# Requesting nine of fourteen weight pieces behind the gather of expert 0, and another order of the first low halves

## The chip, the cores and the metric
The kernel runs on one core of a Trainium2 chip. The metric is the device time of one execution in microseconds (us). The core has five engines that run their own instruction streams side by side: TensorE (PE, with its weight loads shown as PEld), VectorE (DVE), ScalarE (ACT), GpSimd (POOL) and SyncE (SP). SP issues most of the DMAs here; all its loads go into one hardware queue in the order in which it issues them.

## The reference
Three stages in a row, all in float32:

```
# gated linear attention, B=2, H=8, S=768, D=48
state = alpha[t] * state + outer(k[t], v[t]);  y[t] = q[t] @ state
x = y as [1536 tokens, 384]

# mixture of experts, top 1 of 8, capacity 384
logits = x @ w_gate;  e = argmax(logits)
gate = exp(logits - max) / (sum + 1e-9)      # of the chosen expert
h = relu(rows_of_expert @ w1[e])             # 384 -> 1024
out[token] = gate * (h @ w2[e])              # 1024 -> 384

# feed-forward
h = out @ w_in                               # 384 -> 2048
g = h * tanh(softplus(h))
result = g @ w_out                           # 2048 -> 384
```

## The kernel before
**Attention** runs in 12 tiles of 128 tokens. As tiles end, POOL scatters their token rows (1,536 B each) into a table `tab` in DRAM, sorted by expert (line 108). `gather(e)` (lines 120 to 128) then asks SP for the first 240 rows of expert e's part of the table, in two transfers of 128 and 112 rows (line 124); it waits for the scatters. For expert 0 the gather is issued before the last two tiles are scattered; their rows are put in by TensorE (`slot_mm`, `slot_rest`).

**The expert loop** has 64 steps, 8 experts with 8 blocks of 128 hidden units each. Step s does `g1` of block s (9 matmuls, line 1063: high half of the weights by high half of the rows, low by high, high by low), ScalarE and VectorE split the result into `hh` and `hl` (lines 1067, 1068), and `g2` of the block three steps back follows (9 matmuls, line 1080). At block 5 of each expert `xpose` turns the next expert's rows (TensorE, line 1035, straight behind that step's `g2`), and the gather of the expert after that is asked for.

**The weights** come in pieces of 384 KB, numbered in the order of use: an even piece is `w1` for two blocks, an odd piece `w2` for the same two. Blocks 0 and 1 use pieces 0 and 1, blocks 4 and 5 pieces 4 and 5. Each goes through three steps: `load_to` asks SP for it (line 331) into one of 14 buffers, `conv_high` makes its high half `whi` on ScalarE (line 343), `conv_low` its low half `wlo` on VectorE (line 349: piece minus high half). The weights of the feed-forward come as 64-bit words; `cvt_load` asks for them in 512 KB loads (line 225), the first three of them between the end of attention and the expert loop, and ScalarE and VectorE turn them in spare moments of the loop.

**What sets the order** around the change. The program order is the order of each engine's queue. The table `PRE` says how many pieces are asked for by the end of each attention tile; at tile 11 the lines `load_to(PRE[i])`, `conv_high(1)`, `gather(0)`, `load_to(14)` follow each other. `conv_high(n)` itself asks for pieces up to `ahead[0]` beyond the one it converts. Behind attention come the three `cvt_load`s, the rows of expert 0, the scatter of the last tile and `gather(1)`; requests that `conv_high` makes there stand between them. In the loop, each step calls `conv_high` and `conv_low`; `low` is the list of pieces whose high half is done and low half is not. `places()` computes on VectorE where each expert's tokens begin and `sort_places()` each token's place; POOL scatters the token numbers (`toks`) to these places later.

Of the kernel before, what the change touches and what calls it, by code (L numbers as in the profile page):

```python
# [23 lines left out]
def kernel(  # L24
# [22 lines left out]
    E = w1.shape[0]  # L47
# [18 lines left out]
    ATT = 4  # L66
# [4 lines left out]
    LEAD = 6  # L71
    WST = 6
# [11 lines left out]
    def w_new(i):  # L84
        p = wr_p[2 if i >= 76 else (i + 8) % 12 < 8]
        whi[i], wlo[i] = (p.tile([128, PW], F32R, tag=t, name=f"{t}{i}") for t in ("whi", "wlo"))
# [99 lines left out]
    NP1 = 2 * FF // 256  # L186
# [35 lines left out]
    def cvt_load(n):  # L222
        if n < len(cvt_jobs):
            t = words(fpool[0].tile([128, 2 * CN], F32, tag="big", name="w64", bufs=3)[:, 0:2 * cvt_jobs[n][1].shape[1]])
            nc.sync.dma_start(out=t, in_=words(cvt_jobs[n][0]))
            cvt_t[n] = [t]
# [39 lines left out]
    def late_load(n):  # L266
        if not 0 <= n < NLATE:
            return
        st = late_pool(n).tile([128, PW], F32, tag="st", name=f"sd{n}")
        fs = slice(FH + n // 2 * 128, FH + (n // 2 + 1) * 128)  # L270
        if n % 2:
            nc.sync.dma_start(out=words(st), in_=words(w_out[fs, :]))
        else:
            nc.sync.dma_start(
                out=st.bitcast(U32).rearrange("p (k f) -> p k f", k=KD),
                in_=w_in.bitcast(U32)[:, 2 * fs.start:2 * fs.stop].rearrange("(k p) f -> p k f", p=128),
            )
        late_t[n] = st
# [39 lines left out]
            hi, lo, w = late_t.pop(n)[3:]  # L318
            nc.vector.tensor_tensor(out=lo, in0=w, in1=hi.bitcast(F32), op=ALU.subtract)

    ahead = [WST + 4]
    conv_n, load_n, cvt_n = [0], [0], [0]

    def written(i):
# [2 lines left out]
    def load_to(n):  # L327
        while load_n[0] < min(n, len(pieces)) and cvt_n[0] >= written(load_n[0]):
            i = load_n[0]
            st = raw_p[i % 14 >= 8].tile([128, PW], F32, tag="st", name=f"st{i}")  # L330
            nc.sync.dma_start(out=st.rearrange("p (a b) -> p a b", b=pieces[i].shape[2]), in_=pieces[i])
            wst_t[i] = st
            load_n[0] += 1

    low = []

    def conv_high(n):
        while conv_n[0] < min(n, len(pieces)):
            i = conv_n[0]
            load_to(i + 1 + ahead[0])  # L340
            w = wst_t.pop(i)
            w_new(i)
            nc.scalar.activation(out=whi[i], in_=w, func=AF.Copy)  # L343
            low.append((i, w))
            conv_n[0] += 1

    def conv_low(n=None):
        for i, w in low[:n]:
            nc.vector.tensor_tensor(out=wlo[i], in0=w, in1=whi[i].bitcast(F32), op=ALU.subtract)  # L349
        del low[:n]  # L350

    def conv_to(n):
        conv_high(n)
        conv_low()
# [10 lines left out]
    with ExitStack() as actx:  # L365
# [135 lines left out]
        def decay_check(i):  # L501
            j1 = sp.tile([128, HP, C], F32, tag="junk", name="junk", bufs=1)
            nc.scalar.activation(
                out=j1[0:R2], in_=er_t.pop(i)[0:R2], func=AF.Square, bias=neg1[0:R2], accum_out=chk[0:R2, i:i + 1]
            )
# [254 lines left out]
        def route_c(i):  # L760
            xg = xg_t.pop(i)
            scatter(tab, si_all[:, i:i + 1], xg.rearrange("p j d -> p (j d)"), E * NT, "tab")
# [58 lines left out]
        def slot_mm(i, ks=range(KD)):  # L821
            x = xg_l[i - SLOT1].rearrange("p j d -> p (j d)")
            for kk in ks:
                t = feat(0, WIN)[kk]
                nc.tensor.matmul(  # L825
                    out=t, lhsT=x[:, kk * 128:(kk + 1) * 128], rhs=hot_t[i], start=(i == SLOT1 and kk % 2 == 0),
                    stop=(i == NTILE - 1), skip_group_check=True,
                )
# [63 lines left out]
            for f in (route_lg, route_max, route_exp, route_idx, route_hot):  # L892
                f(i)

        PRE = {5: 1, 6: 3, 7: 5, 8: 8, 9: 11, 10: 12, 11: 12}
        EXP = {4: groups[0], 7: groups[1], 9: groups[2]}
        HOT = {5: groups[0], 7: groups[1], 9: groups[2]}
        RANK = {6: groups[0], 8: groups[1], 10: groups[2]}
        for i in range(1, NTILE - 1):
# [63 lines left out]
            if not far:  # L963
                route_x(i - 1)
                route_c(i - 1)
            load_to(PRE.get(i, 0))
        i = NTILE - 1
# [21 lines left out]
        decay_check(i)  # L989
        load_to(PRE[i])  # L990
        conv_high(1)
        gather(0)
        load_to(14)
        i = NTILE - 1
# [15 lines left out]
        count(i + 1)  # L1010
        route_c(SLOT1)
        conv_high(ATT - 1)
        conv_low(1)
        low.reverse()
        slot_mm(NTILE - 1)
        del xs_t[0]
        tot = rk[:, E:2 * E]
# [38 lines left out]
    def g1(e, m):  # L1056
        xh, xl = xt_e[e]
        wh, wl = w_first(e, m)
        hps = bk[2 + m % 2][:, m // 2 % 2 * WB:m // 2 % 2 * WB + WIN]
        n = 0  # L1060
        for a, b_ in ((wh, xh), (wl, xh), (wh, xl)):
            for kk in range(KD):
                nc.tensor.matmul(out=hps, lhsT=a[:, kk], rhs=b_[:, kk, :], start=(n == 0), stop=(n == 3 * KD - 1))  # L1063
                n += 1
        hh = fp.tile([128, WIN], F32R, tag="hh", name="hh", bufs=LAG + 1)
        hl = fp.tile([128, WIN], F32R, tag="hl", name="hl", bufs=LAG + 1)
        nc.scalar.activation(out=hh, in_=hps, func=AF.Relu)  # L1067
        nc.vector.scalar_tensor_tensor(  # L1068
            out=hl, in0=hps, scalar=0.0, in1=hh.bitcast(F32), op0=ALU.max, op1=ALU.subtract
        )  # L1070
        h_t[e, m] = (hh, hl)

    def g2(e, m):
        y = feat(4 + e % 2 * 2, WIN)
        hh, hl = h_t.pop((e, m))
        wh, wl = w_second(e, m)
        for n in range(KD):
            ns = slice(n * 128, (n + 1) * 128)
            for t, (a, b_) in enumerate(((wh, hh), (wl, hh), (wh, hl))):
                nc.tensor.matmul(  # L1080
                    out=y[n], lhsT=a[:, ns], rhs=b_, start=(m == 0 and t == 0 and n % 2 == 0),
                    stop=(m == MF - 1 and t == 2), skip_group_check=True,
                )
# [15 lines left out]
    def y_out(e):  # L1099
        y_put(4 + e % 2 * 2, off_v.pop(e), free=e == E - 1)  # L1100

    def tok_scatter(i):
        scatter(toks, pos_i[:, i:i + 1], tokid[:, i:i + 1], NT)

    def place(col, engines=DYN):
        return nc.values_load(meta_i[0:1, col:col + 1], engines=engines, min_val=0, max_val=NT)
# [8 lines left out]
    def slow_at():  # L1115
        nc.vector.scalar_tensor_tensor(
            out=slow_f, in0=mxc[0:1], scalar=float(WIN), in1=bad, op0=ALU.is_gt, op1=ALU.max
        )
# [113 lines left out]
    def at(n):  # L1232
        return steps[n] if 0 <= n < NS else None


    def f_mish(n, between=None):
# [22 lines left out]
        if n % 2:  # L1259
            late_low(late - 2)  # L1260
            late_join(late - 1)
            late_load(late + LATE_AHEAD - 1)
        conv_to(E * MF - EARLY + n + LEAD)

# [35 lines left out]
        part(last, cs[3], True)  # L1300

    EARLY = LAG2
    for n in range(3):
        cvt_load(n)
    CVT_END = 45
    LATE_AHEAD = 3
    xpose(0, False)
    nc.vector.tensor_reduce(out=mxc, in_=tot, axis=AX.X, op=ALU.max)
    conv_low(1)
    conv_high(ATT)  # L1310
    scatter(tab, si_last, xg_last, E * NT, "tab")
    gather(1)
# [6 lines left out]
    for e in range(E):  # L1319
        for m in range(MF):  # L1320
            step = e * MF + m
            if m == 6:
                off_v[e] = place(e)
            g1(e, m)
            pend.append((e, m))
            if len(pend) > LAG:
                pe, pm = pend.pop(0)
                g2(pe, pm)
                if pm == MF - 1:
                    y_out(pe)  # L1330
            if e == E - 1 and m >= MF - EARLY:
                n = m - MF + EARLY
                (f_head if m < MF - 1 else f1_at)(n)
            conv_high(min(step + 1 + LEAD, ATT + step * 9 // 8, E * NP1 + 3))
            conv_low(None if step > 2 else min(step, 1))
            for f, n in job_at.get(step, ()):
                f(n)
                if f is cvt_b:
                    cvt_load(n + 3)
            if step == 3:  # L1340
                check_all(cm)
                slow_at()
            if step == 1:
                places()
            if step == 2:
                sort_places()
            if step % 4 == 3 and 0 < step // 4 <= NTILE:
                tok_scatter(step // 4 - 1)
            if e == E - 1 and m == 0:
                nc.sync.dma_start(  # L1350
                    out=srt, in_=toks.rearrange("(c p) o -> p (c o)", p=128), allow_slow_non_contiguous=True
                )
            if E * MF - EARLY - 1 - LATE_AHEAD <= step < E * MF - EARLY - 1:
                late_load(step - (E * MF - EARLY - 1 - LATE_AHEAD))
            if step == E * MF - 4:
                cvt_marks()
            if step == E * MF - 2:
                cvt_flag()
            if m == 5 and e + 1 < E:
                xpose(e + 1)  # L1360
                if e + 2 < E:
                    gather(e + 2)
    for pe, pm in pend:
        g2(pe, pm)
    apart.append(at(EARLY))
    f1(at(EARLY))
# [239 lines left out]
```

## Time and profile before

| | |
|---|---|
| median of 3 runs | 425.91 us (425.75 to 427.06) |
| the profiled execution | 426.99 us, its span 424.8 us |
| TensorE busy | 409.5 us, 96% of the span |
| VectorE busy | 324.7 us, 76% |
| ScalarE busy | 324.5 us, 76% |
| DMA, mean over the span | 158 GB/s |

The profile is of one execution; the span is from the first to the last instruction, and 2.2 us of the execution lie around it. Attention ends and the expert loop begins at about 80 us. A window row gives for a stretch the busy time of each engine, the clock that TensorE was granted (1.00 is 2.4 GHz, 0.50 is 1.2 GHz), the mean busy share of the 16 DMA engines (it can come out a little over 1) and the rate. In a timeline, a row with xN groups N instructions in a row, and brackets give the idle time of the engine before it and what ended it.

### The profile page before, as it was taken

What the parts mean: (1) busy time and instruction counts of PE and PEld (TensorE: products, weight loads), DVE (VectorE), ACT (ScalarE), POOL (GpSimd) and SP (SyncE); (2) the same over time, 40 slices, a digit from 0 to 9 for tenths busy, and PEclk for the clock granted to TensorE, in tenths of its full rate; (3) what the DMA queues carried; (4) which work ended last, traced back from release to release, by engine and by line L of the source; (5) the groups of instructions that cost most, each with busy time, mean ns of one, the idle gap of its engine ahead of it and who ended that gap; (6) DMA issues with size and microseconds to landing.
All of it is one profiled execution on the core that took longest, in us unless ns stands there. A gap on an engine that the chain in (4) does not pass through costs nothing.

```text
span 424.8 us, 8347 instructions
## 1 busy us (share of the span) xinstructions
PE 409.5 (96%) x3110; PEld 377.2 (89%) x3112; DVE 324.7 (76%) x643; ACT 324.5 (76%) x571; POOL 59.8 (14%) x76
## 2 busy tenths in 40 slices
PE   7899998989999999999999999999999999999993
PEld 3798977889999999999988989898989998889893
DVE  7999985699898988988749877966796675565451
ACT  5889977667778776877679988788878878797640
POOL 5222564221120111100000000000000000002033
PEclk9999997899999999999999999999999999999998
DMA  8999995799999999971552300112110000001022
GB/s 237 350 291 329 363 378 186 248 294 299 320 315 275 295 280 322 279 238 27 179 181 71 115 1 0 39 41 72 37 39 3 0 2 0 0 2 75 2 76 79
DMA packets 50541, 67.31 MB, mean 158 GB/s; under 512 B 5372, under 2 KB 41212, under 8 KB 50492
## 3 DMA queue, kind: packets, MB, share of 16 engines
q1 hardware_dynamic: 48572, 61.97, 48.1%
q0 software_dynamic: 1920, 4.73, 3.0%
q8 instruction: 26, 0.43, 0.4%
q14 instruction: 23, 0.19, 0.1%
HBM read 55.86 MB, written 10.83 MB: 157 GB/s over the span
## 4 chain that ended last, share of the span: by engine, by line
PE 91%; DVE 3%; issue 1%; ACT 1%; POOL 1%; DMA 1%; SPq 0%; POOLq 0%; DVEq 0%; ACTq 0%
PE bk L1144 24%; PE bk L1187 23%; PE bk L1080 15%; PE bk L1063 15%; PE bk L526 3%; PE bk L572 3%; PE bk L588 3%; PE bk L561 2%; PE bk L540 1%; PE bk L1035 1%; PE bk L596 1%; DMA kn<-in_k_t_dram 1%; DVE wlo L349 1%; PE bk L825 1%; POOL st__990 L531 0%
## 5 line engine op out<-in xcount | busy, mean ns | idle before, releaser
L349 DVE TENSOR_TENSOR wlo<-st,whi 128x768 fp32r<-128x768 f32 x72 | 68.3, 954 | 13.1 <-ACT whi L343 10.8
L1187 PE MATMUL bk<-whi,big 128*128 128x384 f32 x240 | 66.4, 337 | 0.0
L1172 DVE TENSOR_TENSOR p<-p,bk 128x512 f32<-128x512 f32 x48 | 32.8, 683 | 43.2 <-ACT p L1162 43.2
L343 ACT ACTIVATE whi<-st 128x768 fp32r<-128x768 f32 x72 | 60.1, 840 | 0.0
L1156 ACT ACTIVATE p<-bk 128x512 f32<-128x512 f32 x48 | 28.8, 599 | 31.9 <-PE bk L1144 28.6
L1080 PE MATMUL bk<-hl,whi 128*128 128x240 f32 x192 | 52.9, 276 | 0.0
L1080 PE MATMUL bk<-hh,wlo 128*128 128x240 f32 x192 | 52.7, 275 | 0.0
L1080 PE MATMUL bk<-hh,whi 128*128 128x240 f32 x192 | 52.7, 274 | 0.0
L1187 PEld LDWEIGHTS bk<-whi,big 128*128 128x128 f32 x240 | 44.1, 188 | 1.5
L108 POOL DMA_INDIRECT out_dram<-acc,srt x12 | 12.2, 1017 | 235.0 <-DVE acc L1211 230.6
L1067 ACT ACTIVATE hh<-bk 128x240 fp32r<-128x240 f32 x64 | 23.5, 368 | 28.3 <-PE bk L1063 28.3
L1144 PE MATMUL bk<-x2l,whi 128*128 128x512 f32 x144 | 41.6, 397 | 0.0
L1144 PE MATMUL bk<-x2h,wlo 128*128 128x512 f32 x144 | 41.2, 394 | 0.0
L1144 PE MATMUL bk<-x2h,whi 128*128 128x512 f32 x144 | 41.1, 394 | 0.0
L1187 PE MATMUL bk<-wlo,big 128*128 128x384 f32 x120 | 40.6, 338 | 0.0
L1080 PEld LDWEIGHTS bk<-hl,whi 128*128 128x128 f32 x192 | 36.4, 189 | 0.2 <-DVE hl L1068 0.2
L1080 PEld LDWEIGHTS bk<-hh,whi 128*128 128x128 f32 x192 | 36.3, 189 | 0.0
L1080 PEld LDWEIGHTS bk<-hh,wlo 128*128 128x128 f32 x192 | 36.3, 189 | 0.0
L1063 PE MATMUL bk<-xh,wlo 128*128 128x240 f32 x192 | 32.0, 275 | 1.7 <-DVE wlo L349 1.7
L1063 PE MATMUL bk<-xh,whi 128*128 128x240 f32 x192 | 32.9, 280 | 0.4 <-ACT xh L1052 0.4
L1144 PEld LDWEIGHTS bk<-x2h,wlo 128*128 128x128 f32 x144 | 27.0, 188 | 6.7
L1144 PEld LDWEIGHTS bk<-x2l,whi 128*128 128x128 f32 x144 | 27.0, 188 | 6.4
(230 smaller groups left out, 963.1 us busy)
## 6 DMA issues: line engine op xcount, KB each, us to landing
st<-in_w_dram SPq DMA_DIRECT2D x64, 384.0 KB
qn<-in_q_t_dram SPq DMA_DIRECT2D x12, 256.0 KB
kn<-in_k_t_dram SPq DMA_DIRECT2D x12, 256.0 KB
w<-in_w_in_dram SPq DMA_DIRECT2D x6, 512.0 KB
w<-in_w_out_dram SPq DMA_DIRECT2D x6, 512.0 KB
sd<-in_w_in_dram SPq DMA_DIRECT2D x8, 384.0 KB
sd<-in_w_out_dram SPq DMA_DIRECT2D x8, 384.0 KB
tab<-zero SPq DMA_DIRECT2D x4, 720.0 KB
```

The costliest lines, as they stand in the source:

```text
L343: nc.scalar.activation(out=whi[i], in_=w, func=AF.Copy)
L349: nc.vector.tensor_tensor(out=wlo[i], in0=w, in1=whi[i].bitcast(F32), op=ALU.subtract)
L526: nc.tensor.matmul(out=sc_t[i][r][:, j], lhsT=kp[p, j, :], rhs=qq[p, j, :], start=True, stop=True)
L572: nc.tensor.matmul(out=ot_at(j, r), lhsT=vn[:, h * D:h * D + w], rhs=st[:, r, j, :], start=(i % NC_B == 0 and j % 2 == 0), stop=True, skip ...
L588: nc.tensor.matmul(out=xb[:, j, 0:SW], lhsT=xt[0:R2, j, :], rhs=sel[0:R2, j, :], start=True, stop=True)
L1063: nc.tensor.matmul(out=hps, lhsT=a[:, kk], rhs=b_[:, kk, :], start=(n == 0), stop=(n == 3 * KD - 1))
L1067: nc.scalar.activation(out=hh, in_=hps, func=AF.Relu)
L1080: nc.tensor.matmul(out=y[n], lhsT=a[:, ns], rhs=b_, start=(m == 0 and t == 0 and n % 2 == 0), stop=(m == MF - 1 and t == 2), skip_group_ch ...
L1144: r = nc.tensor.matmul(out=hps, lhsT=a[:, kk], rhs=b_[:, kk, w0:w0 + wd], start=(n == 0), stop=(n == 3 * KD - 1))
L1156: nc.scalar.activation(out=p, in_=h2_t[b], func=AF.Sigmoid, scale=-1.0)
L1172: nc.vector.tensor_tensor(out=g, in0=g, in1=h2_t.pop(b), op=ALU.mult)
L1187: nc.tensor.matmul(out=o_t[c], lhsT=a[:, ts], rhs=b_, start=(m in (0, MA) and n == 0), stop=(m in (MA - 1, MF2 - 1) and n == 2),)
```

## The change
Pieces are asked for at another time. `PRE` asks for five pieces by the end of attention instead of twelve, and `ahead` no longer pulls more in at the first conversion; so `load_to(14)` behind `gather(0)` now asks for nine pieces (5 to 13) instead of two. The low halves get another order: piece 0, then 2 ahead of the loop, 1 at step 0, 4 at step 1, 3 at step 2; the high half of piece 4 is made at step 0 instead of step 1. `places` and `sort_places` move from steps 1 and 2 to steps 4 and 5. From the removed line on, line numbers after the change are one lower.

```diff
@@ -318,7 +318,7 @@
             hi, lo, w = late_t.pop(n)[3:]
             nc.vector.tensor_tensor(out=lo, in0=w, in1=hi.bitcast(F32), op=ALU.subtract)
 
-    ahead = [WST + 4]
+    ahead = [ATT]
     conv_n, load_n, cvt_n = [0], [0], [0]
 
     def written(i):
@@ -344,10 +344,10 @@
             low.append((i, w))
             conv_n[0] += 1
 
-    def conv_low(n=None):
-        for i, w in low[:n]:
+    def conv_low(only=None):
+        for i, w in [x for x in low if only in (None, x[0])]:
             nc.vector.tensor_tensor(out=wlo[i], in0=w, in1=whi[i].bitcast(F32), op=ALU.subtract)
-        del low[:n]
+            low.remove((i, w))
 
     def conv_to(n):
         conv_high(n)
@@ -892,7 +892,7 @@
             for f in (route_lg, route_max, route_exp, route_idx, route_hot):
                 f(i)
 
-        PRE = {5: 1, 6: 3, 7: 5, 8: 8, 9: 11, 10: 12, 11: 12}
+        PRE = {6: 1, 7: 2, 8: 3, 9: 4, 10: 5, 11: 5}
         EXP = {4: groups[0], 7: groups[1], 9: groups[2]}
         HOT = {5: groups[0], 7: groups[1], 9: groups[2]}
         RANK = {6: groups[0], 8: groups[1], 10: groups[2]}
@@ -1010,8 +1010,7 @@
         count(i + 1)
         route_c(SLOT1)
         conv_high(ATT - 1)
-        conv_low(1)
-        low.reverse()
+        conv_low(0)
         slot_mm(NTILE - 1)
         del xs_t[0]
         tot = rk[:, E:2 * E]
@@ -1300,13 +1299,14 @@
         part(last, cs[3], True)
 
     EARLY = LAG2
+    FIRST = {0: 1, 1: 4, 2: 3}
     for n in range(3):
         cvt_load(n)
     CVT_END = 45
     LATE_AHEAD = 3
     xpose(0, False)
     nc.vector.tensor_reduce(out=mxc, in_=tot, axis=AX.X, op=ALU.max)
-    conv_low(1)
+    conv_low(2)
     conv_high(ATT)
     scatter(tab, si_last, xg_last, E * NT, "tab")
     gather(1)
@@ -1331,8 +1331,8 @@
             if e == E - 1 and m >= MF - EARLY:
                 n = m - MF + EARLY
                 (f_head if m < MF - 1 else f1_at)(n)
-            conv_high(min(step + 1 + LEAD, ATT + step * 9 // 8, E * NP1 + 3))
-            conv_low(None if step > 2 else min(step, 1))
+            conv_high(ATT + 1 if step == 0 else min(step + 1 + LEAD, ATT + step * 9 // 8, E * NP1 + 3))
+            conv_low(FIRST.get(step))
             for f, n in job_at.get(step, ()):
                 f(n)
                 if f is cvt_b:
@@ -1340,9 +1340,9 @@
             if step == 3:
                 check_all(cm)
                 slow_at()
-            if step == 1:
+            if step == 4:
                 places()
-            if step == 2:
+            if step == 5:
                 sort_places()
             if step % 4 == 3 and 0 < step // 4 <= NTILE:
                 tok_scatter(step // 4 - 1)
```

On SP, at the end of attention, in the kernel before (st is a piece with its number, xs the rows of an expert, tab the table of rows):

```order
-L331 DMA st8_1076<-in_w1_dram 128x3x256
-L331 DMA st9_1078<-in_w2_dram 128x2x384
-L331 DMA st10_1080<-in_w1_dram 128x3x256
-L331 DMA st11_1186<-in_w2_dram 128x2x384
-L124 DMA xs_1267<-tab_77 128x384
-L124 DMA xs_1267<-tab_77 112x384
```

In the changed kernel at the same place, from the last requests of attention on:

```order
+L331 DMA st4_1172<-in_w1_dram 128x3x256
+L124 DMA xs_1253<-tab_77 128x384
+L124 DMA xs_1253<-tab_77 112x384
+L331 DMA st5_1256<-in_w2_dram 128x2x384
+L331 DMA st6_1258<-in_w1_dram 128x3x256
+L331 DMA st7_1260<-in_w2_dram 128x2x384
+L331 DMA st8_1262<-in_w1_dram 128x3x256
+L331 DMA st9_1264<-in_w2_dram 128x2x384
+L331 DMA st10_1266<-in_w1_dram 128x3x256
+L331 DMA st11_1268<-in_w2_dram 128x2x384
 L331 DMA st12_1270<-in_w1_dram 128x3x256
 L331 DMA st13_1272<-in_w2_dram 128x2x384
```

Pieces 5 to 11 moved from in front of the two transfers of the gather to behind them, ahead of pieces 12 and 13.

On VectorE, in the first steps of the expert loop, in the kernel before (wlo is the low half of the piece of that number, hl the low half of a block's result; lines 1110 to 1113 are places, 1122 to 1127 sort_places):

```order
L349 TENSOR_TENSOR wlo1_1317<-st1_784,whi1_1316 128x768
L1110 SCALAR_TENSOR_TENSOR inc_113<-bk7_93,zn_116 128x8
L1111 TENSOR_TENSOR off_114<-inc_113,bk7_93 128x8
L1112 CAST meta_i_106<-off_114 128x8
L1113 SCALAR_TENSOR_TENSOR inc_113<-down_108,off_114 128x8
L1068 SCALAR_TENSOR_TENSOR hl_1417<-bk2_88,hh_1416 128x240
L349 TENSOR_TENSOR wlo3_1363<-st3_876,whi3_1362 128x768
L1122 TENSOR_TENSOR po_1426<-oh_all_137,inc_113 128x96
L1126 TENSOR_REDUCE pk_1428<-po_1426 128x12
L1127 TENSOR_TENSOR pos_i_104<-pk_1428,si_all_107 128x12
L1068 SCALAR_TENSOR_TENSOR hl_1441<-bk3_89,hh_1440 128x240
L349 TENSOR_TENSOR wlo4_1400<-st4_878,whi4_1399 128x768
```

In the changed kernel, from the end of the work ahead of the loop on:

```order
L349 TENSOR_TENSOR wlo2_1320<-st2_972,whi2_1319 128x768
L1067 SCALAR_TENSOR_TENSOR hl_1381<-bk2_88,hh_1380 128x240
L349 TENSOR_TENSOR wlo1_1317<-st1_872,whi1_1316 128x768
L1067 SCALAR_TENSOR_TENSOR hl_1400<-bk3_89,hh_1399 128x240
L349 TENSOR_TENSOR wlo4_1387<-st4_1172,whi4_1386 128x768
L1067 SCALAR_TENSOR_TENSOR hl_1414<-bk2_88,hh_1413 128x240
L349 TENSOR_TENSOR wlo3_1363<-st3_1066,whi3_1362 128x768
L1067 SCALAR_TENSOR_TENSOR hl_1433<-bk3_89,hh_1432 128x240
L349 TENSOR_TENSOR wlo5_1420<-st5_1256,whi5_1419 128x768
L349 TENSOR_TENSOR wlo6_1448<-st6_1258,whi6_1447 128x768
```

The low half of piece 4 moved from behind places, piece 3 and sort_places to just behind piece 1 and one subtraction; places and sort_places are no longer among these rows.

## Rows read from the trace of the kernel before

**Rows 1.** The page, part 1: busy us, share, instructions of each engine.
```profile
PE 409.5 (96%) x3110; PEld 377.2 (89%) x3112; DVE 324.7 (76%) x643; ACT 324.5 (76%) x571; POOL 59.8 (14%) x76
```

**Rows 2.** The page, part 4: the chain that ended last, by line.
```profile
PE bk L1144 24%; PE bk L1187 23%; PE bk L1080 15%; PE bk L1063 15%; PE bk L526 3%; PE bk L572 3%; PE bk L588 3%; PE bk L561 2%; PE bk L540 1%; PE bk L1035 1%; PE bk L596 1%; DMA kn<-in_k_t_dram 1%; DVE wlo L349 1%; PE bk L825 1%; POOL st__990 L531 0%
```

**Rows 3.** Waits of TensorE, 0 to 95 us: total, times, longest.
```profile
PE bk L1063 <- DVE wlo L349: 1.7, 1, 1.7
```

**Rows 4.** Timeline of TensorE, 84 to 93 us: start, length, instruction, [idle before].
```profile
85.93 0.58 PE L1063 MATMUL bk<-xh,whi 128*128 128x240 f32 x3
88.23 0.60 PE L1063 MATMUL bk<-xh,wlo 128*128 128x240 f32 x3 [1.72 <-DVE wlo L349]
...
90.02 0.50 PE L1063 MATMUL bk<-xh,whi 128*128 128x240 f32 x3
...
92.03 0.78 PE L1035 MATMUL bk<-ident,xs 128*128 128x128 f32 x6
```

**Rows 5.** Timeline of VectorE, same columns.
```profile
83.65 0.95 DVE L349 TENSOR_TENSOR wlo<-st,whi 128x768 fp32r<-128x768 f32 x1
84.52 0.16 DVE L1110 TENSOR_TENSOR_SCAN inc<-bk,zn 128x8 f32<-128x8 f32 x1
...
85.39 0.95 DVE L349 TENSOR_TENSOR wlo<-st,whi 128x768 fp32r<-128x768 f32 x1
86.25 0.25 DVE L1122 TENSOR_TENSOR po<-oh_all,inc 128x96 f32<-128x96 bf16 x1
...
86.91 0.40 DVE L1068 SCALAR_TENSOR_TENSOR hl<-bk,hh 128x240 fp32r<-128x240 f32 x1
87.23 2.69 DVE L349 TENSOR_TENSOR wlo<-st,whi 128x768 fp32r<-128x768 f32 x3
```

**Rows 6.** Timeline of SyncE's DMA issues, 69 to 97 us.
```profile
69.52 0.82 SPq L124 DMA_DIRECT2D xs<-tab  x2
...
77.71 1.30 SPq L225 DMA_DIRECT2D w<-in_w_in_dram  x3
79.15 5.85 SPq L331 DMA_DIRECT2D st<-in_w_dram  x3
85.34 0.81 SPq L124 DMA_DIRECT2D xs<-tab  x2
```

**Rows 7.** DMA issues by kind, with the size of one.
```profile
st<-in_w_dram SPq DMA_DIRECT2D x64, 384.0 KB
...
w<-in_w_in_dram SPq DMA_DIRECT2D x6, 512.0 KB
...
xs<-tab SPq DMA_DIRECT2D x8, 192.0 KB
...
xs<-tab SPq DMA_DIRECT2D x8, 168.0 KB
```

**Rows 8.** Windows: us, busy us of PE, PEld, DVE, ACT, POOL, PEclk, DMA share, GB/s.
```profile
55.00:60.00 5.00, 4.70 (x72) 4.01 (x72) 4.22 (x10) 4.97 (x12) 3.93 (x4) 1.00 1.06 385
60.00:65.00 5.00, 4.17 (x50) 3.35 (x48) 4.12 (x16) 3.18 (x9) 3.17 (x5) 1.00 1.01 360
65.00:70.00 5.00, 3.77 (x53) 3.22 (x54) 2.49 (x12) 2.14 (x5) 2.69 (x4) 1.00 0.36 137
70.00:75.00 5.00, 5.00 (x38) 4.28 (x35) 2.36 (x12) 4.84 (x14) 0.85 (x3) 0.51 0.73 217
75.00:80.00 5.00, 5.00 (x28) 4.30 (x27) 3.33 (x16) 2.52 (x7) 2.32 (x2) 0.81 0.41 120
80.00:85.00 5.00, 4.62 (x39) 4.42 (x38) 3.86 (x11) 3.88 (x8) 0.00 (x0) 1.00 0.99 367
85.00:90.00 5.00, 3.28 (x29) 3.06 (x28) 4.93 (x12) 3.36 (x8) 1.76 (x1) 1.00 0.96 298
90.00:95.00 5.00, 5.00 (x47) 5.00 (x46) 4.90 (x12) 3.36 (x7) 0.71 (x1) 1.00 1.04 310
```

**Rows 9.** Timeline of POOL: the last scatter ahead of the gather.
```profile
66.86 0.98 POOL L108 DMA_INDIRECT tab<-xg,si_all  x1 [0.33 <-issue]
```

## The prediction

> **What bounds the kernel now.** I read the page's busy times first: TensorE works 409.5 of 424.8 us [rows 1], so time can be won or lost almost only where TensorE waits. The chain of waits gives VectorE's low halves (line 349) 1% of the span, the only weight step in it that is not TensorE's [rows 2]. The table of TensorE's waits over the first 95 us puts one 1.7 us wait on that line at the top [rows 3]. The timeline shows its place: the first three matmuls of block 4 start at 85.93, the next three, which read the low half of piece 4, at 88.23; undisturbed, a triple takes 0.335 us (six of them, block 5's and block 2's, lie between 90.02 and 92.03) [rows 4]. They could have started at 85.93 + 0.34 = 86.27, so 1.96 us are to be had. VectorE explains it: low half 1 at 83.65, then the four operations of places (from 84.52, 0.16 us each), low half 3 at 85.39, the three of sort_places (from 86.25; the next operation starts at 86.91), and only at 87.23 a run of three low halves that begins with piece 4 [rows 5]. Next I looked at what comes just behind: the transposes of expert 1's rows at 92.03, without a wait [rows 4]. Their rows were requested at 85.34, behind three 512 KB loads and three pieces in the one queue that SP issues loads into [rows 6]. The windows show that queue's state: DMA share 0.99, 0.96, 1.04 from 80 on, but 0.36 in 65:70 and 0.41 in 75:80 [rows 8]. There the change puts more bytes.
>
> **The low halves.** VectorE ends low half 1 at 84.60 [rows 5]. In the new order the low half of piece 4 comes next but for one short subtraction on a block's result, 0.40 us (line 1068 at 86.91 is such a one [rows 5]), so it ends by 84.60 + 0.40 + 0.95 = 85.95, ahead of 86.27. The wait goes in full: −1.96 us, and the transposes could begin at 92.03 − 1.96 = 90.07. Low half 3 is late next; it is used by the second matmuls of block 2, a lag of three blocks behind, and follows piece 4 by one 0.95 us row. Bounds: −1.96 to 0.
>
> **places and sort_places** move to steps 4 and 5. The same seven operations, 4 × 0.16 for the one and 0.66 us for the other [rows 5], about 1.3 us, run later. VectorE is 4.93 of 5 us busy in 85:90 and 4.90 in 90:95 [rows 8], so if nothing covers them there they delay a later half by up to 1.3 us. I take 0, since the wait that I expect at the transposes covers them. The first scatter of token numbers by POOL and the eleven behind it start later by the same two or three steps; they feed the combine stage far behind. 0.
>
> **The high half of piece 4** is made one step earlier, one ScalarE copy of the same size as before. Its cover is ScalarE's idle time (3.36 of 5 us busy in 85:90 [rows 8]). 0; without that cover low half 4 comes late and the 1.96 us stay.
>
> **The requests.** Before, twelve pieces were asked for ahead of the gather of expert 0 and two behind it; now five ahead and nine behind. SP's own issue time is not the matter (two transfers of a gather are issued in 0.82 us [rows 6]); the bytes are. I count what must go through the queue from the gather at 69.52 to the gather of expert 1, by sizes [rows 7]: expert 0's rows 0.37 MB, pieces 12 and 13 0.79, three loads of w 1.57, pieces 14 to 16 1.18, expert 1's rows 0.37, and two scatters of 128 rows of 1,536 B 0.39: 4.67 MB. Check on before: 70:85 moved 5 × (217 + 120 + 367) = 3.52 MB; the remaining 1.15 at 298 GB/s end at 88.9. From the end of bytes to the engine that waits I add 1.7 us, read where a scatter's row ends on POOL at 67.84 and the gather that waits for it is issued at 69.52 [rows 6, 9]. That gives 90.6, and indeed the transposes at 92.03 did not wait. So only 1.4 us of slack are there before anything is added.
>
> Now seven pieces more: 2.75 MB, in all 7.42 MB. Of the idle DMA time some is used: (1 − 0.73) × 5 + (1 − 0.41) × 5 = 4.3 us in 70:80 [rows 8]; 2.75 MB need 7.5 us at 367 and 9.0 at 304 (the mean of 298 and 310). That excess is the cost. In order: start at 71.0 (between the end of the gather's issue at 70.34 and 71.35, where the idle share of 70:75 would put it if it lay wholly in front). Gather, nine pieces and one scatter, 4.10 MB: pieces alone run at about 304, mixed traffic at 367; I take the mean 335, 12.25 us, to 83.25. The loads of w, 1.57 MB at the 367 of 80:85, to 87.5. The second scatter, three pieces and expert 1's rows, 1.75 MB at 304, to 93.3. With 1.7 us: 95.0. Ends: all at 385, the fastest row [rows 8], 71.0 + 19.3 + 1.7 = 92.0; all at 298, 97.6.
>
> TensorE arrives at 90.07 and takes its instructions in order, so behind the first transpose stand blocks 6 and 3 and all that follows, and ScalarE and VectorE, which split each block's result, stand still with it. Wait 95.0 − 90.07 = 4.9 us; against the 1.96 that went, **+3.0 us** (ends 0.0 and +5.6). The backlog goes on in the queue after that. Piece 5 and its neighbours are first behind the gather and used from about 84 us on; I cost their landing at 0, and a late one at no more than the wait itself.
>
> **The clock.** The granted clock was at its lower level (1.2 GHz) in 70:75 (0.51) and for a part of 75:80 (0.81): 4.9 + 1.9 = 6.8 us at half, that is 3.4 us lost. In front of it TensorE had been busy 3.77 of 5 us. In 85:90 it was busy only 3.28 and the clock stayed at 2.4 GHz [rows 8]. A wait of 4.9 us is far longer than either, so a fall is likely but its length open: 0 to +3.4, I take half, **+1.7**. The Trainium skill, "TensorE: Matmul & The Clock Gate", section "HAM oscillation — how this bites in real kernels", describes just this: a DMA wait between groups of matmuls makes the next group start at the lower clock. 70:75 agrees, 85:90 does not show it; by that rule alone the forecast would lie up to 1.7 us above mine.
>
> **The attention stage** has fewer loads in it now. TensorE's longest wait up to 95 us is the 1.7 on VectorE, so none on a load is longer [rows 3]; I take 0. What an earlier end would be worth stands with the third rival.
>
> **Sum.** −1.96 + 4.9 + 1.7 = +4.7. The profiled execution took 426.99 us (1.1 above the median of three), so a profile like it would read 431.7; from the median 425.91 it is **430.6**.
>
> **Rivals.** *One wait for another (not slower, not faster).* If the queue keeps the 385 GB/s of 55:60 throughout, expert 1's rows are there at 92.0, exactly when TensorE began before: 425.9. For it: that stretch carried pieces too. Against it: the rows of 85:90 and 90:95 are at 298 and 310. 0.13.
>
> *The low halves pay in full (faster).* The rows are there by 90.07: 425.91 − 1.96 = 424.0. That needs 7.42 MB in 90.07 − 1.7 − 71.0 = 17.4 us, 427 GB/s, or a first transfer that starts 2 us sooner and the 385. No row reaches 427. The Trainium skill, "DMA: Bandwidth & Descriptors", section "Specifications", gives a fabric ceiling of 435 GB/s, by which it would just be possible; the same table's limit of about 358 per core from HBM would put the rows at 93.4, and the fastest row here, 385, lies between the two. 0.12.
>
> *Shorter attention.* Scatters no longer share the engines with seven pieces. If all of TensorE's idle time in 60:70 went, (5 − 4.17) + (5 − 3.77) = 2.1 us [rows 8], and the low clock after it, 3.4, the gather would be asked for 2.1 us earlier and expert 1's rows come at 92.9, 0.9 after TensorE's 92.03 of now: 426.8, and with the 385 GB/s on top 423.9. Against it: the DMA share of 0.36 in 65:70 says that the scatters in front of the gather were not crowded. 0.09, of which 0.05 faster.
>
> *The change does not remove the wait.* If low half 4 is still behind others (because the high half comes late on ScalarE, behind a copy that waits for a load), 1.7 us stay and the transposes wait 3 instead of 4.9; the end is the same. It is within the forecast.
>
> **How the numbers follow.** Forecast: 0.66, its own range 427.2 (wait 3.3, no fall of the clock) to 433.8 (wait 6.4 and the full 3.4). About 0.3%, 1.28 us, is what a measurement of this kernel can tell from no change; so slower 0.66. The first rival and the 426.8 of the third lie within: same 0.17. The second and the rest of the third: faster 0.17. For 8 in 10 the range goes down to the second rival's 424.0, leaving out the third's 423.9 and the tail above: 424.0 to 433.8.
>
> **What would show it.** No wait on line 349 at the second triple of block 4, and low half 4 right behind low half 1: the first step. The first transpose of expert 1 with a wait on its rows (xs), ending between 92 and 97.6: the second; DMA share near 1.0 from 71 to 95 without the gap of 75:80, and the request of expert 1's gather again near 85. A granted clock under 1.00 in the stretch behind that wait: the third. I am wrong if the first transpose starts at 90 without a wait, if the DMA rate in 71:83 lies near 400, or if the attention stage ends at another time than now.

## The result and the profile after

The changed kernel takes 432.62 us, median of 6 runs (432.19 to 433.38), beside 426.68 us of the kernel before (425.75 to 427.63, 6 runs): 1.4% slower, ratio 1.0141 with a 95% interval of 1.0121 to 1.0162. The forecast was 430.6. In the profiled executions the span went from 424.8 to 430.1 us. Here and below, ratios and intervals are of executions within 1.5% of the fastest of the same kernel, so they need not be the quotient of the two medians; of those left out one stands far off, at 578 us with a granted clock of 0.656.

Waits of TensorE in the changed kernel (total, times, longest), against the one wait of [rows 3]:

```profile
PE bk L1034 <- DMA xs<-tab: 4.6, 1, 4.6
...
PE bk L1062 <- DVE hl L1067: 1.7, 1, 1.7
```

The wait on low half 4 is gone, and two others stand in its place. Their position, in TensorE's timeline of the changed kernel (start, length, instruction, idle before; lines behind the edit are one lower):

```profile
78.52 0.64 PE L1062 MATMUL bk<-xh,whi 128*128 128x240 f32 x3 [0.38 <-ACT xh L1051]
...
83.78 0.60 PE L1062 MATMUL bk<-xh,whi 128*128 128x240 f32 x3 [1.70 <-DVE hl L1067]
...
85.92 0.58 PE L1062 MATMUL bk<-xh,whi 128*128 128x240 f32 x3
86.34 0.50 PE L1062 MATMUL bk<-xh,wlo 128*128 128x240 f32 x3
...
94.84 1.48 PE L1034 MATMUL bk<-ident,xs 128*128 128x128 f32 x6 [4.63 <-DMA xs<-tab]
96.00 0.97 PE L1062 MATMUL bk<-xh,whi 128*128 128x240 f32 x3
...
99.66 0.50 PE L1062 MATMUL bk<-xh,whi 128*128 128x240 f32 x3
```

Block 4's triples now start at 85.92 and 86.34, without a wait, where [rows 4] had 85.93 and 88.23. Expert 1's transposes start at 94.84, after 4.63 us of waiting for their rows, where [rows 4] had 92.03 and no wait. One more row of before, from block 7:

```profile
94.68 0.50 PE L1063 MATMUL bk<-xh,whi 128*128 128x240 f32 x3
```

From the transposes on the changed kernel is 94.84 − 92.03 = 2.81 us late, at block 7, two blocks further, 99.66 − 94.68 = 4.98. In between nothing is waited for; the matmuls are slower. The windows of the changed kernel show why (columns as in [rows 8]):

```profile
70.00:75.00 5.00, 4.40 (x43) 3.47 (x38) 3.35 (x18) 4.88 (x16) 0.84 (x3) 1.00 0.84 228
75.00:80.00 5.00, 4.54 (x34) 4.17 (x34) 3.60 (x15) 3.67 (x7) 2.25 (x2) 1.00 0.94 301
80.00:85.00 5.00, 3.30 (x28) 3.02 (x27) 3.30 (x7) 2.41 (x5) 0.00 (x0) 1.00 1.07 389
85.00:90.00 5.00, 5.00 (x47) 4.97 (x45) 4.90 (x11) 4.36 (x9) 0.00 (x0) 1.00 1.03 388
90.00:95.00 5.00, 0.37 (x3) 0.17 (x3) 3.48 (x11) 0.34 (x1) 0.97 (x1) 0.75 1.09 327
95.00:100.00 5.00, 5.00 (x28) 4.84 (x29) 1.95 (x4) 1.93 (x4) 0.00 (x0) 0.57 1.13 376
```

The DMA engines are busy 0.94 in 75:80, where [rows 8] has 0.41, and 1.03 and more behind it; the rate is 389 and 388 GB/s in 80:90. TensorE is busy 0.37 of 5 us in 90:95, and the granted clock falls to 0.75 and 0.57, its lower level (1.2 GHz) for 2.5 + 4.3 = 6.8 us, of which a part lies behind 94.84. The issues on SP, against [rows 6]:

```profile
69.56 0.81 SPq L124 DMA_DIRECT2D xs<-tab  x2
70.42 7.04 SPq L331 DMA_DIRECT2D st<-in_w_dram  x9
77.62 1.73 SPq L225 DMA_DIRECT2D w<-in_w_in_dram  x3
80.22 3.38 SPq L331 DMA_DIRECT2D st<-in_w_dram  x3
84.35 2.01 SPq L124 DMA_DIRECT2D xs<-tab  x2
```

The gather of expert 0 is issued at 69.56, as before (69.52), and the gather of expert 1 at 84.35, even earlier than 85.34. Only what stands in front of it in the queue is more: nine pieces between 70.42 and 77.46 instead of two.

### The profile page after: what moved, and what is told of

It is laid out like the page before. It is cut to its first block, busy times and chain, and to the rows that moved or that the text cites. A ratio compares the mean times of both kernels' runs of the same rounds, so it can differ in the third digit from the quotient of the medians.

```text
span 430.1 us, 8349 instructions
## 1 busy us (share of the span) xinstructions
PE 410.0 (95%) x3110; PEld 376.9 (88%) x3112; DVE 324.3 (75%) x643; ACT 324.1 (75%) x571; POOL 59.1 (14%) x76
## 4 chain that ended last, share of the span: by engine, by line
PE 86%; DMA 6%; DVE 2%; SPq 1%; issue 1%; ACT 1%; POOL 1%; POOLq 0%; DVEq 0%
PE bk L1143 23%; PE bk L1186 23%; PE bk L1079 15%; PE bk L1062 14%; PE bk L526 3%; DMA xs<-tab 2%; PE bk L572 2%; DMA st<-in_w_dram 2%; PE bk L561 2%; PE bk L588 1%; PE bk L1034 1%; PE bk L540 1%; SPq L331 1%; DMA kn<-in_k_t_dram 1%; PE bk L596 1%
## 5 line engine op out<-in xcount | busy, mean ns | idle before, releaser
L1067 DVE SCALAR_TENSOR_TENSOR hl<-bk,hh 128x240 fp32r<-128x240 f32 x64 | 25.7, 402 | 9.3 <-ACT hh L1066 9.3
```

The lines of the kernel that those rows point to most:

```text
L1067: nc.vector.scalar_tensor_tensor(out=hl, in0=hps, scalar=0.0, in1=hh.bitcast(F32), op0=ALU.max, op1=ALU.subtract)
```

## The experiments

The profiles differ in where attention ends. In the eight profiles from two of the chips used, the first matmul of the expert loop comes at 74.5 to 74.9 us; in the six others it comes at 77.4 to 80.5. The four profiles of the two unedited kernels are all among the six, so an early end of the kernel before is not shown, but its times on one of the two chips run from 421 to 428 us. So times are compared with the kernel before in the same set of runs only, and positions are counted from the issue of expert 0's gather in the same profile; this distance is what the experiments on the requests are read by.

**The order alone.** The changed kernel with the requests of before:

```diff
-    ahead = [ATT]
+    ahead = [WST + 4]
-        PRE = {6: 1, 7: 2, 8: 3, 9: 4, 10: 5, 11: 5}
+        PRE = {5: 1, 6: 3, 7: 5, 8: 8, 9: 11, 10: 12, 11: 12}
```

> The new order of the low halves, places and sort_places later and the high half of piece 4 a step earlier, with the requests as in the kernel before (twelve pieces ahead of expert 0's gather). Theory 'late rows' (the changed kernel is slower because expert 1's rows land behind seven more pieces): TensorE reaches the first transpose at about 90.1 and the rows, 192 KB and 168 KB asked for near 85, are there within 1 us of it: no wait or a short one, 1.0 to 2.0 us faster than before (424.7 to 425.7). Rival 'order' (the earlier high half of piece 4 holds ScalarE up until block 3's matmuls wait for a hidden half, 1.7 us, and places at steps 4 and 5 crowd VectorE): slower than before by 1 us or more.

Measured: 424.56 us beside 425.37, ratio 0.9961 (0.9916 to 1.0005): not slower, a gain not shown. Its profile has the side effect that "order" spoke of. ScalarE's timeline, and TensorE's:

```profile
76.08 0.37 ACT L1066 ACTIVATE hh<-bk 128x240 fp32r<-128x240 f32 x1 [0.48 <-PE bk L1062]
81.23 0.84 ACT L343 ACTIVATE whi<-st 128x768 fp32r<-128x768 f32 x1 [4.78 <-DMA tab<-xg_l,si_all]
81.98 0.61 ACT L1066 ACTIVATE hh<-bk 128x240 fp32r<-128x240 f32 x2
```

```profile
82.83 1.00 PE L1062 MATMUL bk<-xh,whi 128*128 128x240 f32 x3 [4.61 <-DVE hl L1067]
...
90.61 0.78 PE L1034 MATMUL bk<-ident,xs 128*128 128x128 f32 x6
```

The high half of piece 4, a step earlier than before, stood 4.78 us for the landing of a scatter of attention's last rows; behind it stood the high part of block 1's result, and block 3's matmuls waited 4.61 us. The transposes at 90.61 did not wait for their rows. So the order is not what makes the changed kernel slower, but it carries a wait of its own.

**The requests alone.** The kernel before with `PRE` and `ahead` of the changed one (the reverse of that diff).

> The requests of the changed kernel (five pieces ahead of expert 0's gather, nine behind) with the low halves, places and sort_places in the order of before. 'Late rows': expert 1's transposes begin at 94.8 again whatever TensorE did before, as the queue sets it; the wait is 2.8 us or more, the time within 1 us of the changed kernel's (+4 to +6 us over before). Rival 'order': the time is that of before to within 1 us.

Measured: 429.55 us beside 425.37, ratio 1.0101 (1.0014 to 1.0188): slower. The issue of expert 0's gather on SP, and TensorE's timeline:

```profile
67.48 1.54 SPq L124 DMA_DIRECT2D xs<-tab  x2
```

```profile
83.32 0.60 PE L1063 MATMUL bk<-xh,wlo 128*128 128x240 f32 x3 [2.09 <-DVE wlo L349]
...
92.28 1.46 PE L1035 MATMUL bk<-ident,xs 128*128 128x128 f32 x6 [3.38 <-DMA xs<-tab]
```

The old wait on low half 4 is there (2.09 us), and behind it 3.38 us for the rows: they come 92.28 − 67.48 = 24.8 us after the gather of expert 0 was issued, in the changed kernel 94.84 − 69.56 = 25.3. "Late rows" said 94.8 flat; it is the distance that holds, and the start that moves.

**The high half of piece 4 back at step 1**, in the changed kernel:

```diff
-            conv_high(ATT + 1 if step == 0 else min(step + 1 + LEAD, ATT + step * 9 // 8, E * NP1 + 3))
+            conv_high(min(step + 1 + LEAD, ATT + step * 9 // 8, E * NP1 + 3))
```

> The changed kernel with the high half of piece 4 back at step 1. 'Late rows': the 1.7 us wait of block 3 that stood on that copy goes, and TensorE only comes to the transposes earlier; the rows land at the same time, so the time is that of the changed kernel to within 0.7 us (432 to 433). 'Order': 1 to 2 us faster than the changed kernel.

Measured: 430.39 us beside 424.45, ratio 1.0108 (1.0015 to 1.0200). The time lies 2 us under the one expected and near what "order" expected, but the changed kernel itself was not run beside it, and in this profile the gather was issued at 67.41. So the distance has to tell:

```profile
67.41 1.46 SPq L124 DMA_DIRECT2D xs<-tab  x2
```

```profile
92.75 1.48 PE L1034 MATMUL bk<-ident,xs 128*128 128x128 f32 x6 [6.87 <-DMA xs<-tab]
```

92.75 − 67.41 = 25.3 us, the changed kernel's distance to a tenth. TensorE came earlier and waited longer, 6.87 us. So the wait on that copy costs the changed kernel nothing: the rows come when they come.

**Expert 1's gather ahead of pieces 14 to 16**, in the changed kernel:

```diff
-    conv_high(ATT)
     scatter(tab, si_last, xg_last, E * NT, "tab")
     gather(1)
+    conv_high(ATT)
```

> The changed kernel, but expert 1's gather is asked for ahead of pieces 14 to 16 instead of behind them (the scatter it waits for goes ahead of the high half of piece 3). 'Late rows': 1.18 MB less stand in front, 3.6 us at 327 GB/s, so the rows are there near 91.2 and the wait falls from 4.6 to about 1 us, the clock does not fall: about 6 us less than the changed kernel, 425.5 to 427.5. Rival 'order': nothing changes. Rival 'clock alone' (the low clock behind the wait is what counts): between, some 2 us less.

Measured: 424.54 us beside 425.37, ratio 0.9996 (0.9959 to 1.0033): against the median of the kernel before the loss is gone with one moved request, and the time is 1 us under the range expected for a later end of attention.

```profile
67.28 1.49 SPq L124 DMA_DIRECT2D xs<-tab  x2
```

```profile
89.19 1.01 PE L1034 MATMUL bk<-ident,xs 128*128 128x128 f32 x6 [0.49 <-DMA xs<-tab]
```

The transposes start 89.19 − 67.28 = 21.9 us after expert 0's gather, 3.4 us less than in the changed kernel (3.6 were expected), with a wait of 0.49. Block 3 still waited 2.44 us behind the high half of piece 4.

**Nine pieces ahead and five behind**, in the changed kernel:

```diff
-    ahead = [ATT]
+    ahead = [WST + 2]
-        PRE = {6: 1, 7: 2, 8: 3, 9: 4, 10: 5, 11: 5}
+        PRE = {5: 1, 6: 3, 7: 4, 8: 6, 9: 8, 10: 9, 11: 9}
```

> The changed kernel with nine pieces ahead of expert 0's gather and five behind it (instead of five and nine). 'Late rows', as a matter of bytes: four pieces less, 1.57 MB, 4.1 to 5.2 us at 385 to 304 GB/s, so expert 1's rows land about 4.5 us earlier and the wait at the transposes falls from 4.6 to 5.1 us to 0 to 0.6, without a fall of the clock: 424 to 426, a step down of 6 to 8 us. If the number of pieces does not matter in this way (a single late request, or the order): 431 to 433.

Measured: 424.16 us beside 424.45, ratio 1.0001 (0.9957 to 1.0046).

```profile
67.19 1.60 SPq L124 DMA_DIRECT2D xs<-tab  x2
```

```profile
80.88 0.79 PE L1062 MATMUL bk<-xh,whi 128*128 128x240 f32 x3 [2.74 <-DVE hl L1067]
...
88.78 0.78 PE L1034 MATMUL bk<-ident,xs 128*128 128x128 f32 x6
```

No wait for the rows at the transposes, 88.78 − 67.19 = 21.6 us after expert 0's gather, so the rows were there 3.7 us or more earlier than in the changed kernel; the number of pieces is what matters. The wait at 80.88 is again the one behind the high half of piece 4, and the granted clock was 0.66 in 80:85 behind it. So it is not shown that nothing of the cost is left: eleven of the 25 executions of the kernel before beside this run took 421.0 to 421.6 us and ten took 426.7 or more, while all ten of this run took 423.1 to 425.5. If the short ones are those in which attention ends early, as it does in this profile (74.57), some 3 us are still lost against them by the medians (424.2 less 421 to 422); no profile shows such an execution of the kernel before.

**TensorE kept busy through the wait**, the changed kernel with 20 and with 12 added matmuls:

```diff
+            if e == 1:
+                for _ in range(NBUSY):
+                    nc.tensor.matmul(out=bk[0], lhsT=busy[:, 0:128], rhs=busy, start=True, stop=True)
             xpose_pe(xs_t.pop(e))
```

> The changed kernel with 20 matmuls of 512 columns on a constant in front of the transposes of expert 1, so that TensorE works through most of the 4.6 us wait (added work: their results are overwritten). 'Late rows' with the clock as its second part: the transposes still begin near 94.8, but at the full clock, so the 2.2 us lost behind the wait come back: 430 to 431. If the clock does not follow activity during the wait: no gain, 432.5 to 433.

Measured with 20: 428.17 us beside 425.37, ratio 1.0088 (1.0043 to 1.0133). TensorE's timeline and the windows:

```profile
89.17 4.49 PE L1049 MATMUL bk<-busy 128*128 128x512 bf16 x20
93.50 0.78 PE L1034 MATMUL bk<-ident,xs 128*128 128x128 f32 x6
94.05 0.58 PE L1065 MATMUL bk<-xh,whi 128*128 128x240 f32 x3
```

```profile
90.00:95.00 5.00, 5.00 (x31) 3.10 (x30) 1.91 (x6) 0.78 (x2) 0.98 (x1) 1.00 1.09 338
95.00:100.00 5.00, 5.00 (x47) 5.00 (x46) 4.00 (x8) 3.78 (x9) 0.00 (x0) 1.00 1.09 322
```

The clock stays at 1.00, and from the transposes to the next block it takes 0.55 us (94.05 − 93.50) where the changed kernel needed 1.16. Twenty were too many: they ended at 93.5 and the transposes followed without a wait, so part of the time won went into them. The time lies under the 430 to 431 expected, but attention ended early here and the changed kernel was not run beside it; what is shown is that the clock held, not what that gains in time.

> The changed kernel with 12 instead of 20 matmuls on a constant in front of expert 1's transposes, added work of about 2.7 us by the 4.49 us of 20, so that it ends ahead of the rows. 'Late rows' with the clock as its second part: the transposes start when the rows land, as in the changed kernel (94.8 to 95.3 where attention ends near 80), but the clock stays at its upper level, so 2 us less than the changed kernel: 430 to 431. If a wait of 2 us left over suffices for a fall of the clock: 432 to 433.

Measured with 12: 428.81 us beside 424.45, ratio 1.0103 (1.0051 to 1.0155).

```profile
67.96 0.81 SPq L124 DMA_DIRECT2D xs<-tab  x2
```

```profile
93.12 1.16 PE L1034 MATMUL bk<-ident,xs 128*128 128x128 f32 x6 [2.46 <-DMA xs<-tab]
```

```profile
95.00:100.00 5.00, 5.00 (x32) 5.00 (x31) 2.57 (x5) 2.17 (x6) 0.00 (x0) 0.66 1.02 265
```

The transposes start 93.12 − 67.96 = 25.2 us after the gather, and 2.46 us of waiting were left: that sufficed for the clock to fall (0.66 in 95:100). The expectation's second case came true in the profile; its times were for an attention that ends near 80.

**Both kernels again**, on another chip, without an edit.

> The kernel before itself, profiled again, because in the first four experiments attention ended about 4 us earlier than in the two profiles so far and the kernel before ran between 421 and 427 us beside them. If the early end is a matter of the execution and not of the edits, this profile shows it either way: with an end near 80 a time near 426.5, with an end near 75 and no long wait for the scatters a time near 421 to 423.

Measured: 425.49 us beside 425.05, ratio 1.0005 (0.9978 to 1.0031), with an end of attention near 79 and low half 4's wait of 1.72 as in [rows 4].

> The changed kernel itself, on the same chip. 'Late rows': where attention ends 4 us earlier the gather of expert 0 is asked for 2.2 us earlier (67.3 as in the profile with expert 1's gather ahead of the pieces), so expert 1's rows land near 92.5 and the time is some 2 us lower than 432.6 only, while the kernel before gains up to 5: the change then costs more there than 1.4%. If 'order' is the cause, the difference to before stays at 6 us.

Measured: 432.62 us beside 425.05, ratio 1.0165 (1.0113 to 1.0218). Attention ended near 80 in this profile, so the case with the earlier end was not met here. The transposes waited 5.05 us and started at 95.41, 26.0 us after the gather:

```profile
69.45 0.81 SPq L124 DMA_DIRECT2D xs<-tab  x2
```

```profile
95.41 1.48 PE L1034 MATMUL bk<-ident,xs 128*128 128x128 f32 x6 [5.05 <-DMA xs<-tab]
```

**Versions that could beat both.** The order alone with the high half of piece 4 back at step 1 (the diff of "The order alone" and that of "The high half of piece 4 back at step 1" together):

> The order alone (requests as before) with the high half of piece 4 back at step 1. In the order-alone run that copy stood 4.8 us on ScalarE for the landing of the next to last scatter, and block 3's matmuls 4.6 us behind it. If the earlier place of the copy is what cost that, the wait shrinks by the 1.0 us of a step or goes over to block 4 in part: 0.5 to 1.5 us faster than the order alone, 1 to 2 us faster than before in the same state of attention. If the scatter's landing sets it alone, no gain: the wait only moves to block 4.

Measured: 423.83 us beside 425.05, ratio 0.9961 (0.9936 to 0.9987): faster than before by 0.4%, and 8.8 us under the changed kernel of the same set of runs.

```profile
68.52 0.81 SPq L124 DMA_DIRECT2D xs<-tab  x2
```

```profile
88.12 1.14 PE L1034 MATMUL bk<-ident,xs 128*128 128x128 f32 x6 [0.84 <-DMA xs<-tab]
```

Now it is the rows that bound it, by 0.84 us, 88.12 − 68.52 = 19.6 us after expert 0's gather, with two pieces in between instead of nine. With expert 1's gather ahead of the pieces as well:

> The same, and expert 1's gather asked for ahead of pieces 14 to 16. 'Late rows': the rows are there before TensorE comes, so no wait at the transposes; the time is that of the run before it or up to 1 us less, and 2 us or more under the kernel before in the same state of attention.

Measured: 424.00 us beside 425.05, ratio 0.9966 (0.9938 to 0.9993): 1 us under the kernel before where 2 or more were expected, and no further gain shown, though the transposes no longer waited; where the 0.8 us went was not followed. With the third 512 KB load behind the gather instead:

```diff
-    for n in range(3):
+    for n in range(2):
         cvt_load(n)
...
     gather(1)
+    cvt_load(2)
```

> The order alone with the high half of piece 4 at step 1, and the third of the three 512 KB loads asked for behind expert 1's gather. 'Late rows': 0.52 MB less in front, 1.4 to 1.7 us, so the 0.8 us wait at the transposes that stood in the run without this goes: 0.3 to 0.8 us faster than it, 1.5 to 2.5 us under the kernel before.

Measured: 423.04 us beside 424.45, ratio 0.9958 (0.9902 to 1.0015). The wait is gone and the median is the lowest of all, but the interval takes in no gain; it is not shown to beat the version before it.

## Why the prediction was right

**The rows of expert 1.** The step that carried the forecast held: TensorE at the transposes at 90.07, rows at 95.0, wait 4.9; measured 94.84 and 4.63, with TensorE there at about 90.2, and in the second profile 95.41 and 5.05. The requests alone give it, four pieces fewer in front (nine ahead, five behind) or three fewer (14 to 16 moved behind) take it away, and with all nine behind the distance from expert 0's gather is 24.8 to 26.0 us in five profiles, whenever TensorE arrives. The sum of bytes came out, its parts less so. Up to 93.14, the 1.7 us of the sum ahead of the transposes, the engines moved 339 GB/s × 22.14 us = 7.5 MB from 71.00 on, where I had 7.42 up to 93.3; but 314 GB/s up to 83.25 and 370 behind it, where I had 335 and some 330, so two errors in the rates cancelled. The windows count all transfers, so how many of these bytes stood in front of the rows is not shown, nor is the 1.7 us for this transfer.

**The clock.** +1.7 was half of a bound, not a reading; 4.98 − 2.81 = 2.2 us is what the trace shows, and it does not come when TensorE is kept busy to the end of the wait. The Trainium skill, "TensorE: Matmul & The Clock Gate", section "HAM oscillation — how this bites in real kernels", says that a DMA wait between groups of matmuls makes the next group start at the lower clock. The windows 90:95 and 95:100 (0.75, 0.57) agree. The 70:75 of the kernel before, which I had counted as agreeing, does not bear on it: TensorE's longest wait in 62:71 was 1.15 us, on VectorE and not on a DMA.

**The low halves.** Low half 4 is done in time in both profiles of the changed kernel, but only in the second in the way that I worked out. VectorE in the first:

```profile
80.67 0.95 DVE L349 TENSOR_TENSOR wlo<-st,whi 128x768 fp32r<-128x768 f32 x1
83.32 0.41 DVE L1067 SCALAR_TENSOR_TENSOR hl<-bk,hh 128x240 fp32r<-128x240 f32 x1 [1.70 <-ACT hh L1066]
83.64 0.95 DVE L349 TENSOR_TENSOR wlo<-st,whi 128x768 fp32r<-128x768 f32 x1
```

Low half 1 ends at 81.62, low half 4 at 84.59, ahead of block 4's 86.34; but they do not follow each other closely, since the subtraction between them came late, at 83.32. In the second profile they do:

```profile
82.50 0.95 DVE L349 TENSOR_TENSOR wlo<-st,whi 128x768 fp32r<-128x768 f32 x1
...
83.78 0.95 DVE L349 TENSOR_TENSOR wlo<-st,whi 128x768 fp32r<-128x768 f32 x1
```

There the expert loop began at 80.35, as I had assumed, and TensorE reached the transposes 95.41 − 5.05 − 80.35 = 10.01 us later, against 92.03 − 80.49 = 11.54 in the kernel before: 1.53 of the 1.96 us are gained. In the first profile it took 94.84 − 4.63 − 78.52 = 11.69 us, so the new order gained nothing there; that TensorE still came at 90.2, near my 90.07, is luck, since attention ended 1.97 us earlier than I had assumed. places and sort_places ran from 91.15 to 93.62 in that profile, inside the wait, as forecast.

**The high half of piece 4** is the step that failed. ScalarE in the first profile:

```profile
79.94 0.37 ACT L1066 ACTIVATE hh<-bk 128x240 fp32r<-128x240 f32 x1 [0.48 <-PE bk L1062]
82.19 0.84 ACT L343 ACTIVATE whi<-st 128x768 fp32r<-128x768 f32 x1 [1.87 <-DMA st<-in_w_dram]
82.94 0.61 ACT L1066 ACTIVATE hh<-bk 128x240 fp32r<-128x240 f32 x2
```

I had costed it at 0, its cover ScalarE's idle time in 85:90, though the copy comes at about 82, and for the loss of that cover I named a late low half 4. What the runs show is another place and another size: the copy waits for a DMA (1.87 us here, 0.17 in the second profile, 4.78 on the scatter in the order-alone run), the split of block 1's result stands behind it, and block 3 waits 1.70 us, not at all, or 4.61 us. In the changed kernel the wait for the rows swallows it; without that wait it eats what the order gains, and the granted clock can fall behind it, as in the run with nine pieces ahead. My fourth rival had a high half that comes late on ScalarE, but as its price the old wait on low half 4. The release printed for the 1.87 us is a load, but piece 4 had been asked for by 54.5 us; in the order-alone run and in both runs with added matmuls the trace prints the scatter for the same copy (4.78, 3.29 and 2.11 us). That it is the scatter here too is argued from these runs, not shown.

**Attention** was taken at 0, and its ending at another time was one of my signs of being wrong. The first profile after met it: the loop began at 78.52 instead of 80.49, without the low clock in 70:80. It is not the cause, because the changed kernel's second profile has the low clock again, and the spans of the two are within 1 us of each other (430.1 and 431.0). The second profile:

```profile
70.00:75.00 5.00, 5.00 (x35) 4.22 (x32) 2.33 (x12) 4.67 (x14) 1.50 (x2) 0.50 0.78 226
75.00:80.00 5.00, 4.97 (x28) 4.15 (x26) 3.06 (x15) 2.62 (x6) 1.46 (x1) 0.81 1.00 318
```

**The sum.** +4.7 was forecast; 2.81 + 2.17 = 4.98 stands at block 7, 5.3 in the span, 5.9 between the medians. Where the last 0.3 us of the span come from was not followed. Of the rivals, "one wait for another" had the rate right in part (388 in 80:90) but not throughout, "the low halves pay in full" fell with the landing at 94.84, and "shorter attention" was met in other profiles, with the requests of before as well (74.66 in the order-alone run), so the change does not bring it; with nine pieces behind the gather the rows still decided.

## What to carry to other kernels

Before moving requests behind another in one queue, follow the queue on to the next request that the bottleneck waits for, and count the bytes in front of it; slack in buffers says nothing about that one. A copy that is moved forward is moved ahead of what stands behind it on its engine: ask what its first wait is, and who waits for the instruction that it now holds up. And when the first wait on a path goes, read the landing time of the next item before counting the gain: here, even with the requests of before, the rows came 0.84 us after TensorE once the wait on low half 4 was gone.

## What the runs showed of the hardware

In the expert loop TensorE's granted clock fell behind waits of 1.94, 2.44, 2.74 and 3.12 us (each time 0.66 in 80:85, in the runs with 12 added matmuls, with expert 1's gather ahead, with nine pieces ahead and with 20 added matmuls) and of 4.63 us (0.57 in 95:100 of the changed kernel); it stayed at 1.00 behind 1.70 us in the changed kernel and behind 1.72 us in the kernel before [rows 4, 8]. The length of one wait does not decide alone: in attention the clock fell to 0.51 in 70:75 of the kernel before, where TensorE's longest wait in 62:71 was 1.15 us, and stayed at 1.00 in the changed kernel's first profile, where it was 1.43. What else decides was not tried.

A scatter by POOL released its reader, the gather of expert 0, 1.7 us after its instruction ended where the DMA share was 0.36 [rows 6, 8, 9]. In the order-alone run, with a DMA share of 0.98 in 75:80, ScalarE stood until 81.23 for one of two scatters whose instructions had ended at 74.21 and 75.49, 5.7 us or more.

The expert loop began at 74.5 to 74.9 us in all eight profiles of two chips and at 77.4 to 80.5 in six others, whichever requests the kernel made. As no kernel was profiled in both groups, what sets the end of attention stays open.
